# Two casts moved in the start-up of an attention and swish kernel: one v cast ahead of two evacuations on ScalarE, one weight cast from GpSimd to VectorE

## Chip, cores, metric

The kernel runs on one core of one Trainium2 chip. The metric is the device time of one execution in microseconds (us). Before the change it is 283.29 us, the median of 3 runs (283.11 to 283.29). The execution that the profiler took was a slower one, 283.81 us.

## The reference, cut to what matters

```python
# attention, 8 batches x 8 heads, 576 rows, head_dim 64
q_s = exp(q - max(q)) ; q_s = q_s / (sum(q_s, -1) + 1e-9)
k_s = exp(k - max(k, 2)) ; k_s = k_s / (sum(k_s, 2) + 1e-9)
kv  = einsum('bhsd,bhse->bhde', k_s, v)
x   = einsum('bhsd,bhde->bhse', q_s, kv)       # then (4608, 512)
# swish layer, d_model 512, d_ff 2048
h = x @ w_in
g = h * (1 / (1 + exp(-beta * h)))
out = g @ w_out                                # float32
```

## The kernel before: the parts concerned

TensorE computes, batch by batch, `h = x @ w_in` (line 457) and `acc = g @ w_out` (line 509). While the weights are still arriving, batch 0 is worked; then the attention of batch 1 is prepared. All weights and inputs arrive as fp32 and are cast to bf16, in the order in which SyncE issues their transfers:

```python
    for k0 in range(4):
        load_w_in(0, k0, k0 + 1)
    for blk in range(1, 4):
        load_w_in(blk, 0, 2)           # 512 KB: k-slices 0 and 1
        load_w_in(blk, 2, 4)           # 512 KB: k-slices 2 and 3
    for j0 in range(0, NJ, 2):
        load_w_out(j0)
    # ... cut
    for blk in range(1, 4):
        for k0 in (0, 2):
            cast_w_in(blk, k0, nc.gpsimd)      # two casts of 128x512
    for j0 in range(0, NJ, 2):
        cast_w_out(j0, nc.gpsimd)
        if j0 == 6:
            # loads of batch 1: q (2), then k, v, v for each half (g)
```

The preparation of batch 1. `b_mm(m)` puts m matmuls of `g @ w_out` between the steps:

```python
    def batch_1():
        b_mm(32)
        eq_exp(1, 0)                     # ScalarE: exp of q, first half
        eq_exp(1, 1)
        eq_sum(1, 0)                     # VectorE: reduce, reciprocal
        eq_div(1, 0, nc.vector)          # VectorE: divide
        for c in range(2):
            ek_exp(1, 0, c)              # ScalarE: exp of k
        b_mm(20)
        eq_sum(1, 1)
        eq_t(1, 0, "X0", None)           # TensorE: "first transposes"
        ev_cast(1, 0, 0, nc.gpsimd)
        ev_cast(1, 0, 1, nc.scalar, 0, 4)
        ev_cast(1, 0, 1, nc.gpsimd, 4, KT9)
        eq_div(1, 1, nc.vector)
        for c in range(2):
            ek_exp(1, 1, c)
        b_mm(3)
        ekv_mm(1, 0, ("H0", "H1"))       # TensorE: first kv group
        b_mm(1)
        eq_t(1, 1, "H2", None)           # TensorE: "second transposes"
        ekv_rk(1, 0)                     # VectorE
        ekv_norm(1, 0, (nc.vector, nc.scalar))
        eq_out(1, 0, nc.vector)          # VectorE: copy of qT
        # ... v casts of the second half, eq_out(1, 1)
        b_mm(4)
        x_group(1, (0,), ["X0", "H0"])   # TensorE
        ekv_mm(1, 1, ("X1", "K"))        # second kv group
        # ... cut; after it the h matmuls of batch 1 begin
```

Finishing a stripe inside `b_mm` also puts its evacuation (line 538, `o<-acc`) into ScalarE's program. The order in which these calls stand is the order in which each engine works.

The softmax here doesn't subtract the row's maximum and nothing guards it: scores larger than these inputs give would overflow.

Of the kernel before, what the change touches and what calls it, by code (L numbers as in the profile page):

```python
# [16 lines left out]
def kernel(  # L17
# [10 lines left out]
    nc = tc.nc  # L28
# [7 lines left out]
    CH = 512  # L36
# [24 lines left out]
    def bank(n, shape, dtype, name):  # L61
        return banks[n].tile(shape, dtype, tag=n, name=name)
# [13 lines left out]
    w_in_b = const.tile([P, KT, FF], BF16, name="w_in_b")  # L76
# [73 lines left out]
    def cast(eng, dst, src):  # L150
        if eng is nc.scalar:
            nc.scalar.copy(dst, src)  # L152
        elif eng is nc.gpsimd:
            if len(src.shape) > 3:
                for i in range(src.shape[1]):
                    cast(eng, dst[:, i], src[:, i])
                return
            n = 1
            for d in src.shape[1:]:
                n *= d  # L160
            nc.gpsimd.affine_select(  # L161
                out=dst, in_=src, pattern=[[0, n]], base=0, channel_multiplier=0,
                compare_op=ALU.is_equal, fill=fill0,
            )
        else:
            eng.tensor_copy(dst, src)  # L166

    def cast_w_in(blk, k0, eng, m0=0, m1=CH):
        t, k1 = ld["wi", blk, k0]
        for k_ in range(k0, k1):  # L170
            cast(eng, w_in_b[:, k_, blk * CH + m0 : blk * CH + m1], t[:, k_ - k0, m0:m1])
# [18 lines left out]
    def eq_exp(b, g):  # L190
        if b not in Eq:
            Eq[b] = atn.tile([P, 2, 2 * NT, 2, D], BF16, tag="Eq", name=f"Eq{b}")
            qz[b] = atn.tile([P, 2, 2 * NT, 2], F32, tag="qz", name=f"qz{b}")
        nc.scalar.activation(  # L194
            Eq[b][:, g].rearrange("p m c d -> p c m d"),
            ld["q", b, g].rearrange("p (c a) (t d) -> p c (a t) d", c=2, t=NT),
            ACTF.Exp,
        )

    def eq_sum(b, g):  # L200
        nc.vector.tensor_reduce(qz[b][:, g], Eq[b][:, g], axis=AX.X, op=ALU.add)  # L201
        nc.vector.reciprocal(qz[b][:, g], qz[b][:, g])

    def eq_div(b, g, eng):
        eng.tensor_tensor(
            Eq[b][:, g],
            Eq[b][:, g],
            qz[b][:, g].unsqueeze(3).to_broadcast((P, 2 * NT, 2, D)),
            ALU.mult,
        )  # L210

    def eq_t(b, g, n, eng):
        if b not in qT:
            qT[b] = atn.tile([P, 2, 2, NT, P], BF16, tag="qT", name=f"qT{b}")
        ps = bank(n, [P, 2 * NT, P], BF16, f"tp{b}_{g}")
        for m in range(2 * NT):
            nc.tensor.transpose(  # L217
                ps[:, m, :], Eq[b][:, g, m].rearrange("p c d -> p (c d)"), ident[:]
            )
        tps[b, g] = ps  # L220
        if eng is not None:
            eq_out(b, g, eng)
# [4 lines left out]
    def ek_exp(b, g, c):  # L227
        if b not in Ek:
            Ek[b] = atn.tile([P, KT9, 2, 2, D], BF16, tag="Ek", name=f"Ek{b}")
        nc.scalar.activation(  # L230
            Ek[b][:, :, g, c],
            ld["k", b, g][:, c].rearrange("p (t d) -> p t d", d=D),
            ACTF.Exp,
        )

    def ve(b):
        return va[b][:, 0 : 2 * KT9].rearrange("p (t g) n -> p t g n", g=2)

    def ev_cast(b, g, c, eng, t0=0, t1=KT9):
        cast(  # L240
            eng,
            ve(b)[:, t0:t1, g, c * VH : c * VH + D],
            ld["v", b, g][:, c, t0 * D : t1 * D].rearrange("p (t d) -> p t d", d=D),
        )
# [21 lines left out]
    def ekv_rk(b, g):  # L266
        for a in range(2):
            j = 2 * g + a
            rks[b, j] = atn.tile([P, 1], F32, tag=f"rk{j}", name=f"rks{b}_{j}")
            nc.vector.reciprocal(rks[b, j][:], ekv[b, j, 0][:, D : D + 1])  # L270
# [12 lines left out]
    def x_out(b, kt, eng):  # L283
        cast(eng, xT[b][:, kt], xps[b, kt][:])
# [207 lines left out]
    def cols(n, st):  # L492

        if n == NCH - 1 and st > 2:
            return ((0, DM // 2), (DM // 2, 3 * DM // 4), (3 * DM // 4, DM))[st - 3]
        return 0, DM

    def b_mm(m):
        while m and pos[0] < len(bq):
            n, st, j = bq[pos[0]]  # L500
            if n * NJ + j + LAG + (n == 1 and j < 4) > done_a[0] and done_a[0] < NCH * NJ - 1 and n:
                break
            if j == 0:
                name = ("X1", "K", "A0", "A1")[st] if n == 0 else f"A{st % 2}"
                if st == 5:
                    name = "X0"
                acc[n, st] = bank(name, [P, DM], F32, f"acc{n}_{st}")
            c0, c1 = cols(n, st)
            nc.tensor.matmul(  # L509
                acc[n, st][:, c0:c1],  # L510
                gs[n, j][:, min(st, 3) * P : (min(st, 3) + 1) * P],
                w_out_b[:, j, c0:c1],
                start=(j == 0),
                stop=(j == NJ - 1),
            )
            if j == NJ - 1 and (n, st) != (0, 3):
                store(n, st)
            pos[0] += 1
            m -= 1

    def store(n, st):
        o = osp.tile([P, DM], F32, tag="o", name=f"o{n}_{st}")
        if n == NCH - 1 and st > 2:
            rows = out[(B - 1) * S : (B - 1) * S + CH, :].rearrange("(p t) e -> p t e", t=NT)
            c0, c1 = cols(n, st)
            if st < 5:
                nc.vector.tensor_scalar(
                    o[:, c0:c1], acc[n, st][:, c0:c1], 0.5, None, op0=ALU.mult
                )
                nc.sync.dma_start(rows[:, 3, c0:c1], o[:, c0:c1])  # L530
            else:
                nc.scalar.activation(o[:, c0:c1], acc[n, st][:, c0:c1], ACTF.Copy, scale=0.5)
                nc.scalar.dma_start(rows[:, 3, c0:c1], o[:, c0:c1])
            return
        if n == 0 and st == 3:
            nc.vector.tensor_scalar(o[:], acc[n, st][:], 0.5, None, op0=ALU.mult)
        else:
            nc.scalar.activation(o[:], acc[n, st][:], ACTF.Copy, scale=0.5)  # L538
        if n == TC:
            for m in range(2):  # L540
                b = 2 * st + m
                nc.sync.dma_start(out[b * S + CH : (b + 1) * S, :], o[m * R : (m + 1) * R])
        else:
            b = n if n < TC else B - 1
            rows = out[b * S : b * S + CH, :].rearrange("(p t) e -> p t e", t=NT)
            nc.sync.dma_start(rows[:, st, :], o[:])
# [87 lines left out]
        unit_mm(0, i, 2, 3)  # L634
    for blk in range(1, 4):
        for k0 in (0, 2):
            cast_w_in(blk, k0, nc.gpsimd)
    for j0 in range(0, NJ, 2):
        cast_w_out(j0, nc.gpsimd)
        if j0 == 6:  # L640
# [13 lines left out]
    def batch_1():  # L654
        b_mm(32)
        eq_exp(1, 0)
        eq_exp(1, 1)
        eq_sum(1, 0)
        eq_div(1, 0, nc.vector)
        for c in range(2):  # L660
            ek_exp(1, 0, c)
        b_mm(20)
        eq_sum(1, 1)
        eq_t(1, 0, "X0", None)
        ev_cast(1, 0, 0, nc.gpsimd)
        ev_cast(1, 0, 1, nc.scalar, 0, 4)
        ev_cast(1, 0, 1, nc.gpsimd, 4, KT9)
        eq_div(1, 1, nc.vector)
        for c in range(2):
            ek_exp(1, 1, c)  # L670
        b_mm(3)
        ekv_mm(1, 0, ("H0", "H1"))
        b_mm(1)
        eq_t(1, 1, "H2", None)
        ekv_rk(1, 0)
        ekv_norm(1, 0, (nc.vector, nc.scalar))
        eq_out(1, 0, nc.vector)
        ev_cast(1, 1, 0, nc.gpsimd)
        ev_cast(1, 1, 1, nc.vector, 0, 3)
        ev_cast(1, 1, 1, nc.scalar, 3, 6)  # L680
        ev_cast(1, 1, 1, nc.gpsimd, 6, KT9)
        eq_out(1, 1, nc.vector)
        b_mm(4)
        x_group(1, (0,), ["X0", "H0"])
        ekv_mm(1, 1, ("X1", "K"))
        x_out(1, 0, nc.scalar)
        ekv_rk(1, 1)
        ekv_norm(1, 1, (nc.vector, nc.scalar))
        x_out(1, 1, nc.vector)
        b_mm(4)  # L690
        store(0, 3)
        x_group(1, (1,), ["H1", "H2"])
        for i in range(4):
            unit_mm(1, i, 0, 1)
        x_out(1, 2, nc.scalar)
        x_out(1, 3, nc.vector)
        for i in range(4):
            unit_mm(1, i, 1, 2)
        for m in range(4):
            q_exp(2, m)  # L700
        unit_mm(1, 4, 0, 2)
        for i in range(5):
            unit_mm(1, i, 2, 3)
        for m in range(3):
            q_norm(2, m)
# [94 lines left out]
```

## Time and profile before

| | before |
|---|---|
| median, range | 283.29 us, 283.11 to 283.29 |
| span of the profiled execution (283.81 us on the clock of the runs) | 282.1 us |
| TensorE | 97% busy, granted clock 1.000 |
| transfers moved from 0 to 42 us | 242 to 406 GB/s, close to saturated |
| two gaps of TensorE that the change aims at | 20.2 to 20.95 us, 42.0 to 42.49 us |

A timeline line gives start, length, engine, source line, operation, output and input tiles, shapes, count and, in brackets, the idle time ahead of it with what ended it. The lines themselves stand in the prediction.

### The profile page before, as it was taken

What the parts mean: (1) busy time and instruction counts of PE and PEld (TensorE: products, weight loads), DVE (VectorE), ACT (ScalarE), POOL (GpSimd) and SP (SyncE); (2) the same over time, 40 slices, a digit from 0 to 9 for tenths busy, and PEclk for the clock granted to TensorE, in tenths of its full rate; (3) what the DMA queues carried; (4) which work ended last, traced back from release to release, by engine and by line L of the source; (5) the groups of instructions that cost most, each with busy time, mean ns of one, the idle gap of its engine ahead of it and who ended that gap; (6) DMA issues with size and microseconds to landing.
All of it is one profiled execution on the core that took longest, in us unless ns stands there. A gap on an engine that the chain in (4) does not pass through costs nothing.

```text
span 282.1 us, 4611 instructions
## 1 busy us (share of the span) xinstructions
PE 273.7 (97%) x1664; PEld 136.2 (48%) x1692; DVE 155.5 (55%) x282; ACT 168.1 (60%) x280; POOL 70.5 (25%) x120
## 2 busy tenths in 40 slices
PE   7989999999999999999999999999999999999995
PEld 3545445545444445444444444444444444444444
DVE  2947359976865485638564766466453333444401
ACT  4856367867965587457854785478454544444411
POOL 3368831450631054104510361027000000000000
PEclk9999999999999999999999999999999999999999
DMA  7999999889799908991699069904200200031112
GB/s 242 371 392 406 388 385 359 291 141 359 176 202 354 209 37 183 326 230 64 141 315 285 34 143 305 279 32 110 79 37 2 76 37 37 2 76 37 40 74 74
DMA packets 51559, 51.69 MB, mean 183 GB/s; under 512 B 21068, under 2 KB 41932, under 8 KB 51536
## 3 DMA queue, kind: packets, MB, share of 16 engines
q1 hardware_dynamic: 51360, 51.33, 60.9%
q8 instruction: 13, 0.21, 0.3%
q14 instruction: 10, 0.08, 0.1%
q10 hardware_dynamic: 144, 0.07, 0.1%
q0 software_dynamic: 32, 0.01, 0.0%
HBM read 38.28 MB, written 9.44 MB: 169 GB/s over the span
## 4 chain that ended last, share of the span: by engine, by line
PE 83%; DMA 13%; ACT 1%; issue 1%; SPq 1%; ACTq 0%
PE acc L509 40%; PE h L457 39%; DMA k<-in_k_dram 7%; DMA wo<-in_moe_w_out_dram 3%; DMA wi<-in_moe_w_in_dram 3%; PE kv L384 2%; PE x L408 2%; PE kv L259 0%; ACT Ek L230 0%; SPq L105 0%; ACT o L538 0%; SPq L117 0%; PE xt L422 0%; PE tp L217 0%; ACT va L152 0%
## 5 line engine op out<-in xcount | busy, mean ns | idle before, releaser
L471 DVE SCALAR_TENSOR_TENSOR g<-th,h 128x512 bf16<-128x512 bf16 x144 | 97.3, 685 | 98.5 <-ACT th L469 98.2
L469 ACT ACTIVATE th<-h,beta_h 128x512 bf16<-128x512 f32 x144 | 97.1, 689 | 85.7 <-PE h L457 82.7
L509 PE MATMUL acc<-w_out_b,g 128*128 128x512 bf16 (+2 forms) x590 | 142.8, 368 | 1.7 <-issue 1.1
L457 PE MATMUL h<-xT,w_in_b 128*128 128x512 bf16 x503 | 127.6, 379 | 1.0 <-POOL w_in_b L161 0.4
L457 PEld LDWEIGHTS <-w_in_b 128*128 128x128 bf16 x576 | 64.8, 113 | 61.9 <-POOL w_in_b L161 1.4
L509 PEld LDWEIGHTS <-g 128*128 128x128 bf16 x608 | 56.9, 98 | 63.9 <-issue 2.5
L315 POOL TENSOR_TENSOR Eq<-Eq,qz 128x512 bf16<-128x512 bf16 x24 | 25.1, 1049 | 84.3 <-issue 41.0
L538 ACT ACTIVATE o<-acc 128x512 f32<-128x512 f32 x34 | 20.0, 591 | 8.9 <-PE acc L509 7.4
L161 POOL TENSOR_SCALAR_AFFINE_SELECT va<-v 128x256 bf16<-128x256 f32 (+3 forms) x55 | 21.6, 427 | 13.8 <-DMA v<-in_v_dram 13.5
L355 ACT ACTIVATE Ek<-k 128x640 bf16<-128x640 f32 x24 | 17.7, 737 | 0.0
L457 PE MATMUL h<-xTt,w_in_b 128*128 128x512 bf16 x63 | 16.4, 379 | 0.1
L313 DVE TENSOR_REDUCE qz<-Eq 128x8 f32<-128x512 bf16 x24 | 16.2, 675 | 0.0
L305 ACT ACTIVATE Eq<-q 128x512 bf16<-128x512 f32 x24 | 14.7, 623 | 0.0
L201 DVE TENSOR_REDUCE qz<-Eq 128x16 f32<-128x1024 bf16 x4 | 4.9, 1216 | 10.8 <-ACT Eq L194 10.8
L166 DVE CAST xT<-x 128x512 bf16<-128x512 f32 x15 | 10.3, 685 | 0.6 <-PE x L408 0.5
L582 PE MATMUL warm<-zf 128*128 128x512 f32 (+1 forms) x14 | 9.0, 778 | 1.5 <-DVE zf L549 1.5
L161 POOL TENSOR_SCALAR_AFFINE_SELECT w_in_b<-wi 128x512 bf16<-128x512 f32 x16 | 9.5, 612 | 3.9 <-DMA wi<-in_moe_w_in_dram 3.8
L152 ACT CAST xT<-x 128x512 bf16<-128x512 f32 x17 | 9.7, 578 | 0.8 <-PE x L408 0.7
L194 ACT ACTIVATE Eq<-q 128x1024 bf16<-128x1024 f32 x4 | 4.2, 1056 | 9.5 <-DMA q<-in_q_dram 9.5
L341 POOL TENSOR_TENSOR Et<-Et,zt 128x512 bf16<-128x512 bf16 x4 | 4.2, 1042 | 21.0 <-DVE zt L340 21.0
L161 POOL TENSOR_SCALAR_AFFINE_SELECT w_out_b<-wo 128x1024 bf16<-128x1024 f32 x8 | 8.3, 1039 | 1.9 <-DMA wo<-in_moe_w_out_dram 1.8
L408 PE MATMUL x<-qT,kvn 64*64 64x512 bf16 x64 | 6.0, 391 | 0.4 <-ACT xT L152 0.4
(52 smaller groups left out, 78.3 us busy)
## 6 DMA issues: line engine op xcount, KB each, us to landing
q<-in_q_dram SPq DMA_DIRECT2D x16, 512.0 KB, 6.2
out_dram<-o SPq DMA_DIRECT2D x31, 256.0 KB, 3.1
k<-in_k_dram SPq DMA_DIRECT2D x24, 320.0 KB, 7.5
v<-in_v_dram SPq DMA_DIRECT2D x24, 320.0 KB, 7.5
wo<-in_moe_w_out_dram SPq DMA_DIRECT2D x8, 512.0 KB, 10.4
wi<-in_moe_w_in_dram SPq DMA_DIRECT2D x6, 512.0 KB, 9.7
k<-in_k_dram SPq DMA_DIRECT2D x4, 576.0 KB, 8.8
v<-in_v_dram SPq DMA_DIRECT2D x6, 288.0 KB, 8.6
```

Source lines behind the costliest of these rows:

```text
L161: nc.gpsimd.affine_select(out=dst, in_=src, pattern=[[0, n]], base=0, channel_multiplier=0, compare_op=ALU.is_equal, fill=fill0,)
L166: eng.tensor_copy(dst, src)
L305: nc.scalar.activation(by_pair(Eq[b], m).rearrange("p t h d -> p h t d"), ld["q", b, hf][:, a : a + 2, :].rearrange("p h (t d) -> p h t d" ...
L313: nc.vector.tensor_reduce(z, e, axis=AX.X, op=ALU.add)
L315: nc.gpsimd.tensor_tensor(e, e, z.unsqueeze(3).to_broadcast((P, NT, 2, D)), ALU.mult)
L355: nc.scalar.activation(Ek[b][:, :, h0:h1, :].rearrange("p t h d -> p h t d"), ld["k", b, hf][:, a : a + h1 - h0, :].rearrange("p h (t d) - ...
L408: nc.tensor.matmul(xps[b, 2 * g + c][o, :], kvn[b][r, j, :], qT[b][r, g, a] if b < EARLY else qT[b][r, :, j, :], start=True, stop=True,)
L457: nc.tensor.matmul(hs[n, i][:], w_in_b[:, kt, blk * CH + r : (blk + 1) * CH : 4], rhs_a(n, kt), start=(kt == 0), stop=(kt == KT - 1),)
L469: nc.scalar.activation(th[:], h[:], ACTF.Tanh, scale=beta_h[:, i // 4, i % 4 : i % 4 + 1])
L471: nc.vector.scalar_tensor_tensor(out=g[:], in0=th[:], scalar=1.0, in1=h[:], op0=ALU.add, op1=ALU.mult)
L509: nc.tensor.matmul(acc[n, st][:, c0:c1], gs[n, j][:, min(st, 3) * P : (min(st, 3) + 1) * P], w_out_b[:, j, c0:c1], start=(j == 0), stop=(j ...
L538: nc.scalar.activation(o[:], acc[n, st][:], ACTF.Copy, scale=0.5)
```

## The change

The intent is to take two short waits off TensorE. Part A: of the second piece of w_in's block 1, VectorE casts k-slice 3 while GpSimd casts slice 2. Part B: ScalarE casts the last piece of v ahead of two evacuations of `acc`, not behind them.

```diff
         for k0 in (0, 2):
-            cast_w_in(blk, k0, nc.gpsimd)
+            if (blk, k0) == (1, 2):
+                t, _ = ld["wi", 1, 2]
+                cast(nc.gpsimd, w_in_b[:, 2, CH : 2 * CH], t[:, 0])
+                cast(nc.vector, w_in_b[:, 3, CH : 2 * CH], t[:, 1])
+            else:
+                cast_w_in(blk, k0, nc.gpsimd)
@@ batch_1 @@
-        b_mm(20)
+        b_mm(6)
+        ev_cast(1, 0, 1, nc.scalar, 0, 4)
+        b_mm(14)
         eq_sum(1, 1)
         eq_t(1, 0, "X0", None)
         ev_cast(1, 0, 0, nc.gpsimd)
-        ev_cast(1, 0, 1, nc.scalar, 0, 4)
         ev_cast(1, 0, 1, nc.gpsimd, 4, KT9)
```

## The prediction

> **What bounds the kernel now.** I read the head of the page first, to see which engine sets the time.
>
> ```profile
> span 282.1 us, 4611 instructions
> PE 273.7 (97%) x1664; PEld 136.2 (48%) x1692; DVE 155.5 (55%) x282; ACT 168.1 (60%) x280; POOL 70.5 (25%) x120
> DMA  7999999889799908991699069904200200031112
> ```
>
> TensorE is busy for 273.7 of 282.1 us, at a granted clock of 1.000, so both parts of the change can only win TensorE's idle time: 8.4 us in the whole run. The DMA digits of 9 in the first six slices (7.05 us each) are the second limit: while the weights and batch 1 arrive, the transfers are saturated. The list of all waits names the two gaps at which the change aims:
>
> ```profile
> PE h L457 <- POOL w_in_b L161: 0.4, 2, 0.2
> PE kv L259 <- ACT va L152: 0.3, 1, 0.3
> ```
>
> The timeline of TensorE from 12.5 us shows where the first lies, and that of GpSimd shows why:
>
> ```profile
> 15.03 5.13 PE L457 MATMUL h<-xT,w_in_b 128*128 128x512 bf16 x23 [0.17 <-issue]
> 20.39 0.41 PE L457 MATMUL h<-xT,w_in_b 128*128 128x512 bf16 x1 [0.23 <-POOL w_in_b L161]
> ...
> 19.72 1.18 POOL L161 TENSOR_SCALAR_AFFINE_SELECT w_in_b<-wi 128x512 bf16<-128x512 f32 x2 [1.72 <-DMA wi<-in_moe_w_in_dram]
> 21.06 1.18 POOL L161 TENSOR_SCALAR_AFFINE_SELECT w_in_b<-wi 128x512 bf16<-128x512 f32 x2 [0.17 <-DMA wi<-in_moe_w_in_dram]
> ```
>
> GpSimd stood idle for 1.72 us until the piece landed at about 19.7, then cast its two k-slices one after the other (612 ns each): slice 2 ready at 20.33, slice 3 at 20.90. TensorE waits for each: one matmul at 20.39, the next at 20.95. Its displayed ends are modelled; from starts, 24 matmuls at 0.216 us from 15.03 give 20.21 as the next free slot, so 0.18 us is lost before slice 2 and 0.56 - 0.216 = 0.34 before slice 3.
>
> The second gap is in the preparation of batch 1. All engines, 36.8 to 45.6 us:
>
> ```profile
> 36.90 1.06 ACT L194 ACTIVATE Eq<-q 128x1024 bf16<-128x1024 f32 x1 [6.18 <-DMA q<-in_q_dram]
> 37.99 1.22 DVE L201 TENSOR_REDUCE qz<-Eq 128x16 f32<-128x1024 bf16 x1 [6.49 <-ACT Eq L194]
> 39.53 1.23 DVE L205 TENSOR_TENSOR Eq<-Eq,qz 128x1024 bf16<-128x1024 bf16 x1
> 40.70 1.21 POOL L161 TENSOR_SCALAR_AFFINE_SELECT va<-v 128x576 bf16<-128x576 f32 x2 [4.21 <-DMA v<-in_v_dram]
> 40.91 0.61 PE L217 MATMUL tp<-ident,Eq 128*128 128x128 bf16 x8
> 41.07 1.06 ACT L538 ACTIVATE o<-acc 128x512 f32<-128x512 f32 x2
> 42.02 0.41 ACT L152 CAST va<-v 128x256 bf16<-128x256 f32 x1
> 42.21 1.22 DVE L205 TENSOR_TENSOR Eq<-Eq,qz 128x1024 bf16<-128x1024 bf16 x1
> 42.49 0.69 PE L259 MATMUL kv<-va,Ek 64*128 64x131 bf16 x18 [0.33 <-ACT va L152]
> 43.11 0.39 PE L509 MATMUL acc<-w_out_b,g 128*128 128x512 bf16 x1
> 43.49 0.62 PE L217 MATMUL tp<-ident,Eq 128*128 128x128 bf16 x8
> 44.16 0.69 DVE L166 COPY qT<-tp 128x1024 bf16<-128x1024 bf16 x1
> 44.91 0.73 PE L408 MATMUL x<-qT,kvn 64*64 64x512 bf16 x4
> ```
>
> The reader is to see two things. ScalarE's cast (42.02 to 42.43) sits behind two evacuations (1.06 us), and TensorE's kv group starts at 42.49, right after it. But VectorE, woken at 37.99 by a q transfer that landed at 36.9, works without a gap until 45.83, and TensorE's transposes start just after its two divisions end (40.76 gives 40.91; 43.43 gives 43.49), as the x group starts just after the copy of qT ends (44.85 gives 44.91). **VectorE's stream, started by the DMA, is the clock of this stage.** The cast is only the last wait in front of one group that lies between two of its ticks.
>
> **What the Trainium skill says.** "TensorE: Matmul & The Clock Gate", the specification table at its head, gives the three other compute engines strict first-in-first-out queues of 8. So the new VectorE cast, which comes before the first multiply (g of unit 0) in that engine's program, will hold that multiply until its transfer has landed. The trace before agrees with in-order engines (the ScalarE cast did wait behind the evacuations). "SBUF — State Buffer", section "Who interferes with whom", says a VectorE copy or cast in a two-port mode takes a port pair that GpSimd also needs, for the whole instruction, and the other engine blocks. "VectorE: DVE Perf Modes", section "The perf-mode tier table", gives 1227 ns for 2048 fp32 elements in SBUF at two per cycle of 0.96 GHz; taking off 1536 elements at 0.52 ns, my estimate for 512 is 0.43 us. No large SBUF cast on VectorE is in this trace (one of 192 elements took 353 ns; 512 from PSUM 685 ns), so mode and lock remain open until the run.
>
> **Part A, the w_in cast.** One 612 ns cast leaves GpSimd; one of about 0.43 us (0.69 at worst) is added to VectorE, beside it. Three cases for the piece that lands at 19.7:
> - No blocking: slice 2 is ready at 20.33 and slice 3 at 20.15. TensorE runs both back to back, 0.34 us earlier.
> - GpSimd first: slice 3 is ready at 20.33 + 0.43 = 20.76 in place of 20.90: 0.14 us.
> - VectorE first: slice 3 at 20.15, slice 2 only at 20.15 + 0.61 = 20.76. The first matmul starts at about 20.82, the second at 21.03, 0.08 us later than now.
>
> The other side of A is the multiplies. In the trace they start at 18.54; the blocked queue lets the first start only at 20.2 (or 20.8). They run at 0.62 us a unit, so g of unit 7, behind seven others and one small operation of 0.5 us, ends about 5.5 us later: 25.7 (or 26.3). It frees the bank into which unit 12 goes. TensorE reaches unit 12 at 20.95 + 23 x 0.216 = 25.92 now, 25.58 in the first case. So there A gives back about 0.15 us, and in the second case 0.5. At 29.4 I expect TensorE between 0.4 us later and 0.3 earlier, most likely 0.1 to 0.2 earlier. GpSimd itself gains nothing: it waits about 0.2 us for each following piece.
>
> And then this is lost: 52 matmuls later TensorE stands before the transposes of Eq, which start at 40.91 because the division ends at 40.76. Now it is free at 29.39 + 52 x 0.216 = 40.62, already 0.29 us early. Being earlier lengthens that wait; being up to 0.29 later only shortens it. **A is worth 0.00 at 40.91.**
>
> **Part B, the v cast.** Nothing is added: the order on ScalarE becomes exp, exp, cast, evacuation, evacuation. The cast runs from about 41.07 to 41.48 instead of 42.02 to 42.43. GpSimd's two v casts end at 41.91, the three matmuls before the kv group leave TensorE free at 41.35 + 3 x 0.216 = 42.00. So kv starts at about 42.0 in place of 42.49: 0.49 us won locally. It takes 0.62 us, one matmul follows (0.22), and at 42.84 TensorE meets the second transposes, whose division still ends at 43.43: it waits 0.65 us there, and starts at 43.49 as before. The two evacuations end at 42.5 as before, in front of an exp that waits for its k transfer until 42.92. **B is worth 0.00 at 43.49.** The sum is 0.0; small shifts downstream (the kv reciprocals are behind the second division in VectorE's queue, so they don't move) I put at 0.1 us.
>
> **Rivals.** First, both gains arrive: 0.34 + 0.49 = 0.8 us, 282.5. The wait list speaks for it, as it blames ScalarE and GpSimd; the ends on VectorE just before 43.49 and 44.91 speak against it. Only a quicker q transfer could move those, and the transfers run at 385 to 406 GB/s whatever the casts do: neither part issues one earlier. Second, the late multiplies become the bound: banks come free 0.5 us or more too late, TensorE passes 40.91 late by more than B's new slack of 0.65 us. That needs almost a microsecond of delay, three times my worst case; it would give 283.5 to 284. Third, the port lock keeps slice 2 back (the third case of A): locally a loss of 0.08, at the end nothing, 283.2.
>
> **Range and chances.** Mechanism says 283.29 less 0 to 0.2; runs before spread over 0.18 us. I say 283.15, with 282.75 below (half of the local gains arrive) and 283.45 above (a bank wait leaks through). A 2% change would be 5.7 us, more than half of all TensorE idle time: 0.5% on each side.
>
> **What would show it.** Right: kv near 42.0 and no wait for the ScalarE cast before it; TensorE idle 0.5 to 0.65 us before the second transposes, which start within 0.1 us of 43.49; x at 44.9; the first multiply at 20.2 to 20.8 behind the VectorE cast. The cast's own length and the start of GpSimd's tell whether they block each other. Wrong: second transposes or x group 0.3 us earlier than now, or a TensorE wait for a multiply near 25.9 that is still there at 43.5.

## The result, and the profile after

The changed kernel takes 283.38 us (median of 4 runs, 283.2 to 283.72) beside 283.29 us before (4 runs by now, 283.11 to 283.45). The ratio is 1.0005 with a 95% interval of 0.9988 to 1.0022. Ratios here and below are the mean time of one kernel's runs over that of the other's of the same rounds, so not quite the ratio of the medians quoted. Executions over 1.5% slower than the fastest of the same kernel are left out of the means.

The head of the page after, and the two lines of its list of waits that answer to the two gaps (engine, line, releaser, us in total, times, longest):

```profile
span 282.0 us, 4639 instructions
PE 276.2 (98%) x1692; PEld 136.3 (48%) x1692; DVE 155.7 (55%) x283; ACT 168.3 (60%) x280; POOL 70.1 (25%) x119
```

```profile
PE tp L217 <- DVE Eq L205: 0.7, 2, 0.4
...
PEld L457 <- POOL w_in_b L161: 0.5, 1, 0.5
```

The rise of TensorE's busy time is not more work: the trace before lacks some matmul records (1664 against 1692). The two waits of before (on POOL and on ACT's `va`) are gone from the list of TensorE's matmuls, and a new one stands there: transposes that wait for VectorE's division of Eq. The wait for the cast of w_in is not gone altogether: one is left in the list of weight loads (PEld).

The timelines of the stage of part A, after (TensorE's matmuls and weight loads, VectorE, GpSimd):

```profile
15.16 11.60 PE L457 MATMUL h<-xT,w_in_b 128*128 128x512 bf16 x52
...
20.52 5.97 PEld L457 LDWEIGHTS <-w_in_b 128*128 128x128 bf16 x29 [0.47 <-POOL w_in_b L161]
...
19.57 0.43 DVE L166 CAST w_in_b<-wi 128x512 bf16<-128x512 f32 x1 [3.58 <-DMA wi<-in_moe_w_in_dram]
19.92 4.26 DVE L471 SCALAR_TENSOR_TENSOR g<-th,h 128x512 bf16<-128x512 bf16 x7
...
19.61 0.86 POOL L161 TENSOR_SCALAR_AFFINE_SELECT w_in_b<-wi 128x512 bf16<-128x512 f32 x1 [1.69 <-DMA wi<-in_moe_w_in_dram]
```

TensorE's matmuls are drawn as one row, but a wait is left in it: 24 of them at 0.216 us from 15.16 end at 20.34, and the weights of slice 2 are loaded only at 20.52, so 0.18 us is lost there; slice 3 follows one matmul later. VectorE's cast takes the 0.43 us of my estimate. GpSimd's cast beside it takes 0.86 us in place of 0.612. The multiplies start at 19.92, behind the cast, in place of 18.54.

The stage of part B, after, all engines:

```profile
36.84 1.06 ACT L194 ACTIVATE Eq<-q 128x1024 bf16<-128x1024 f32 x1 [6.33 <-DMA q<-in_q_dram]
...
40.85 0.61 PE L217 MATMUL tp<-ident,Eq 128*128 128x128 bf16 x8 [0.27 <-DVE Eq L205]
...
41.35 0.41 ACT L152 CAST va<-v 128x256 bf16<-128x256 f32 x1 [0.25 <-DMA v<-in_v_dram]
...
41.66 1.08 ACT L538 ACTIVATE o<-acc 128x512 f32<-128x512 f32 x2
...
42.03 0.69 PE L259 MATMUL kv<-va,Ek 64*128 64x131 bf16 x18
42.15 1.22 DVE L205 TENSOR_TENSOR Eq<-Eq,qz 128x1024 bf16<-128x1024 bf16 x1
...
43.43 0.62 PE L217 MATMUL tp<-ident,Eq 128*128 128x128 bf16 x8 [0.39 <-DVE Eq L205]
...
44.85 0.73 PE L408 MATMUL x<-qT,kvn 64*64 64x512 bf16 x4
```

The cast is ahead of the evacuations and the kv group starts at 42.03 in place of 42.49. The second transposes start at 43.43 in place of 43.49, and that 0.06 is exactly what the q transfer was earlier in this execution (36.84 for 36.90). The won 0.46 us now stands as idle time ahead of the transposes. The chain of waits after (start, us, what) shows the same from behind; before, its piece at this place ran over k's transfer, the evacuations and the v cast:

```profile
26.33 10.49 DMA q<-in_q_dram
...
36.84 1.07 ACT Eq L194
...
42.15 1.24 DVE Eq L205
...
43.43 0.62 PE tp L217 x8
```

### The profile page after: what moved, and what is told of

Its sections match the earlier page's. It is cut to its first block, busy times and chain, and to the rows that moved or that the text cites. A ratio compares the mean times of both kernels' runs of the same rounds, so it can differ in the third digit from the quotient of the medians.

```text
span 282.0 us, 4639 instructions
## 1 busy us (share of the span) xinstructions
PE 276.2 (98%) x1692; PEld 136.3 (48%) x1692; DVE 155.7 (55%) x283; ACT 168.3 (60%) x280; POOL 70.1 (25%) x119
## 4 chain that ended last, share of the span: by engine, by line
PE 84%; DMA 11%; DVE 2%; SPq 1%; ACT 0%; issue 0%; POOL 0%; ACTq 0%
PE acc L509 40%; PE h L457 39%; DMA wo<-in_moe_w_out_dram 4%; DMA q<-in_q_dram 4%; DMA wi<-in_moe_w_in_dram 3%; PE kv L384 2%; PE x L408 2%; DVE Eq L205 1%; DVE qz L201 1%; SPq L105 1%; ACT Eq L194 0%; SPq L117 0%; PE xt L422 0%; POOL w_in_b L161 0%; PE kv L259 0%
## 5 line engine op out<-in xcount | busy, mean ns | idle before, releaser
L509 PE MATMUL acc<-w_out_b,g 128*128 128x512 bf16 (+2 forms) x608 | 145.5, 368 | 0.0
L582 PE MATMUL warm<-zf 128*128 128x512 f32 (+1 forms) x14 | 9.6, 824 | 1.5 <-DVE zf L549 1.5
```

What stands on the lines that cost most here:

```text
L509: nc.tensor.matmul(acc[n, st][:, c0:c1], gs[n, j][:, min(st, 3) * P : (min(st, 3) + 1) * P], w_out_b[:, j, c0:c1], start=(j == 0), stop=(j ...
```

## The experiments

My theory: VectorE's stream in batch 1, started by the q transfer, is the clock of that stage, so local gains of TensorE ahead of its ticks become idle time. Rivals: each part gains and the other part spoils it; or no time was freed at all. Unless told otherwise a run has 5 timed rounds. "Before" in the same rounds was 283.27 us for the first four, 283.35 us for the next four, 283.48 us for the last.

### Each part alone

`a_only` has only the first hunk of the diff, `b_only` only the second.

> Part A alone (one w_in cast on VectorE). Theory (VectorE's stream, started by the q transfer, is the clock of batch 1's preparation): TensorE comes to its first w_out matmul 0.2 to 0.3 us earlier than in the kernel before, then waits longer in front of the transposes of Eq; these start at 40.9 within 0.1 us, the second ones at 43.5, and the time is that of before within 0.1 us. Rival 1 (the gain of 0.3 us arrives): 283.0. Rival 2 (A's later multiplies cost what part B wins, which is why the sum is nothing): 283.6 or more, and a TensorE wait for a multiply near 25.5.

> Part B alone (the v cast ahead of two evacuations). Theory: the kv group starts near 42.0 in place of 42.49, the second transposes at 43.5 as before, with 0.4 to 0.6 us of TensorE idle ahead of them; time as before within 0.1 us. Rival 1 (the gain arrives): 282.8. Rival 2 (A spoils B): faster than before by 0.3 us or more, and faster than A alone.

Measured: 283.36 us (ratio 1.0001, 0.9988 to 1.0013) and 283.30 us (1.0001, 0.9987 to 1.0015). Neither gains, neither costs, so it isn't that one spoils the other. The profiled executions seem to contradict: the span of `b_only` is 281.4 us, 0.7 under before. Its timeline tells why (ScalarE's first exp of q, then TensorE's second transposes):

```profile
36.25 1.06 ACT L194 ACTIVATE Eq<-q 128x1024 bf16<-128x1024 f32 x1 [5.41 <-DMA q<-in_q_dram]
...
42.84 0.62 PE L217 MATMUL tp<-ident,Eq 128*128 128x128 bf16 x8
```

The q transfer came 0.65 us earlier in that execution. Set beside each other, the four traces are one and the same from q on:

| start, us | before | after | a_only | b_only |
|---|---|---|---|---|
| exp of q (transfer landed) | 36.90 | 36.84 | 36.54 | 36.25 |
| second transposes, after q | 6.59 | 6.59 | 6.59 | 6.59 |
| h matmuls of batch 1, after q | 10.68 | 10.68 | 10.63 | 10.67 |
| span, less the start of q's exp | 245.2 | 245.2 | 245.2 | 245.2 |

With or without A or B, the time of these four executions is the landing of q plus a constant, to 0.05 us, and the landing moves by some tenths between executions by itself. (k and v come in the same stream of transfers, so the table alone does not tell which of them holds the stage; the next experiment does.) A comparison of spans would have "shown" a gain of 0.7 us for part B. One expectation missed: in `b_only` TensorE waits not 0.4 to 0.6 but only 0.08 us ahead of the second transposes (42.54 + 0.216 = 42.76, start 42.84), because q was early and TensorE itself late: its first transposes started only when its own 52 matmuls were over, at 29.51 + 52 x 0.216 = 40.74. TensorE's slack in this stage is thus between 0.1 and 0.55 us from one execution to the next.

### VectorE's stream made longer

`sum_twice_after`, the changed kernel:

```diff
+        nc.vector.tensor_reduce(qz[1][:, 1], Eq[1][:, 1], axis=AX.X, op=ALU.add)
         eq_sum(1, 1)
```

> The changed kernel with VectorE's second reduction of Eq (1.21 us) done twice; the result is the same. Theory: VectorE's stream is the clock, so the second transposes move from 43.43 to 44.65, the x group from 44.85 to 46.05, and the time rises by all of 1.2 us, to 284.5. Rival (TensorE, ScalarE or the k transfer is the clock and VectorE has slack like TensorE's 0.6 us): a rise of 0.6 us or less.

Measured: 284.25 us against 283.35 (1.0034, 1.0021 to 1.0046), so +0.9 where the theory said 1.2 and the rival at most 0.6. The trace gives the missing piece. From the landing of q (36.40) the second transposes stand at 7.83 (+1.24, all of it), the x group at 45.65 - 36.40 = 9.25 (+1.24), but the second kv group at 9.64 in place of 8.67 (+0.97). In the kernel before, the x group is halted halfway for ScalarE's normalisation, whose place in ScalarE's stream hangs on k's transfer (weight loads in the trace of before):

```profile
45.23 0.11 PEld L408 LDWEIGHTS <-kvn 64*64 64x64 bf16 x3 [0.22 <-ACT kvn L279]
```

With everything later that halt is gone (the x group takes 0.41 for 0.73 us). So VectorE's stream sets the second transposes and the start of the x group, but not the end of the stage: there ScalarE's stream, held by k's transfer, was the later one, and VectorE had 0.27 us of slack (1.24 less 0.97). The table above agrees: `a_only`'s h matmuls come 0.05 us sooner after q, but counted from the exp of k's second half (42.92, 42.86, 42.51 and 42.25) they start 4.66 or 4.67 us later in all four.

### TensorE made the later one

`pad6_*` puts six needless matmuls ahead of the second transposes, `pad10_*` ten ahead of the first, in both kernels:

```diff
+    def pad(n, m):
+        ps = bank(n, [P, CH], F32, f"pad{m}")
+        for _ in range(m):
+            nc.tensor.matmul(ps[:], ident[:], w_out_b[:, 0, :], start=True, stop=True)
 ...
+        pad("X0", 10)                      # pad10
         eq_t(1, 0, "X0", None)
 ...
         b_mm(1)
+        pad("H2", 6)                       # pad6
         eq_t(1, 1, "H2", None)
```

> The kernel before, with six needless matmuls (1.30 us of TensorE) ahead of the second transposes, so that TensorE and not VectorE is the later one there. Theory: TensorE is free at 43.33, so the transposes move from 43.5 to 44.6, the x group from 44.9 to 45.9, the second kv group from 45.57 to 46.4; the time is 0.8 us above before, 284.1.

> The changed kernel with the same six matmuls. Theory: TensorE was free at 42.87 there, so the transposes go to 44.2, the x group to 45.5, the second kv group to 46.0; the time is 0.4 us above before, 283.7, so 0.45 us faster than the padded kernel before: part B's gain was there as slack and shows as soon as TensorE is the later one. Rival (part B frees no time on TensorE, or gives it back elsewhere): the two padded kernels take the same time.

Measured: 284.32 (1.0036, 1.0024 to 1.0049) and 284.22 us (1.0034, 1.0021 to 1.0046). Their means differ by 0.07 us; the spread of the ten runs makes that -0.1 to 0.25 by my estimate (95%), so the expected 0.45 is a miss. In the traces, TensorE in `pad6_before`, then in `pad6_after`:

```profile
42.08 0.69 PE L259 MATMUL kv<-va,Ek 64*128 64x131 bf16 x18 [0.16 <-ACT va L152]
...
44.44 0.61 PE L217 MATMUL tp<-ident,Eq 128*128 128x128 bf16 x8 [0.27 <-DVE qT L166]
```

```profile
41.83 0.69 PE L259 MATMUL kv<-va,Ek 64*128 64x131 bf16 x18
...
44.19 0.61 PE L217 MATMUL tp<-ident,Eq 128*128 128x128 bf16 x8 [0.27 <-PE acc L509]
```

The h matmuls follow at 48.20 and 47.95. All of the 0.25 us between them stands in front of the kv group already. In `pad6_before` that group still waits for ScalarE's v cast, whose stream follows k's transfer; in `pad6_after` it waits for nothing but TensorE's own matmuls. So part B's gain in this pair is 0.25 us. (The two executions had q at 36.49 and 36.64, so counted from q the h matmuls start at 11.71 and 11.31; but that 0.40 is no fair count, as TensorE in `pad6_after` does not hang on q: its first transposes start at 40.64, right after its own 52 matmuls from 29.40.) This is seen in one pair of traces and not proved by the times. (The padding itself cost about 0.2 us more than its matmuls, in both: the transposes into the same bank start 1.51 us after it, not 1.30.)

> The kernel before with ten needless matmuls (2.16 us) ahead of the first transposes. Theory: TensorE was free at 40.62, so these go from 40.91 to 42.8, the kv group to 43.9, the second transposes to 44.7, the second kv group to 46.45; 0.9 us above before, 284.2.

> The changed kernel with the same ten matmuls. TensorE is later than every other engine up to the x group in both, so only part A's gain can show, and part B's can't. Theory: everything 0.2 to 0.34 us earlier than in the padded kernel before: first transposes 42.5, time 283.9 to 284.0. Rival (A gains nothing on TensorE): the same time.

Measured: 285.12 (284.52 to 285.42; 1.0058) and 285.21 us (285.1 to 285.27; 1.0063). Two misses. The cost is 1.8 us and not 0.6 to 0.9, because I had left out that once TensorE leads, VectorE's reciprocals, normalisation and copy of qT must follow the kv group (they end at 46.73 in `pad10_before`, and the x group starts at 46.78). And part A gains nothing that the times show (the means differ by 0.13 us the wrong way, within the spread). The traces say why: the piece of w_in was cast from 18.92 and 18.60, long before TensorE wanted it, so there was no wait to remove (h matmuls from 16.11 and 15.86 without a gap). I looked at the ten traces taken so far. The cast of this piece begins at 19.5 to 19.7 in before, after and `a_only`, and at 18.4 to 18.9 in the seven others, where TensorE, which then starts its h matmuls up to a microsecond later, has no wait for slices 2 and 3. **The wait that part A attacks is that of some executions**; of the four traces without part A, only that of before has it. The 0.2 us by which after's first w_out matmul was earlier than before's (29.19 for 29.39) was luck to the larger part: part A's share is the 0.07 us found next.

### Part A where its wait always exists

The piece is loaded two transfers later (order 1/0, 2/0, 2/2, 1/2, 3/0, 3/2), in the kernel before, in the changed one, and in one in which VectorE takes slice 2 and GpSimd slice 3. One look each, so state unknown; only the traces are read.

```diff
-    for blk in range(1, 4):
-        load_w_in(blk, 0, 2)
-        load_w_in(blk, 2, 4)
+    for blk, k0 in ((1, 0), (2, 0), (2, 2), (1, 2), (3, 0), (3, 2)):
+        load_w_in(blk, k0, k0 + 2)
 ...                                        # late_swap only:
-                cast(nc.gpsimd, w_in_b[:, 2, CH : 2 * CH], t[:, 0])
-                cast(nc.vector, w_in_b[:, 3, CH : 2 * CH], t[:, 1])
+                cast(nc.vector, w_in_b[:, 2, CH : 2 * CH], t[:, 0])
+                cast(nc.gpsimd, w_in_b[:, 3, CH : 2 * CH], t[:, 1])
```

> The traces so far show that the wait which part A attacks is there in some executions only: the piece landed at 19.7 in the profile of before, but at 18.9 in that of the padded kernels before, where TensorE had no wait. Here the piece is loaded two transfers later (about 22.2), so TensorE always waits for it. The kernel before in this form, counted from the start of GpSimd's first cast of the piece (S): slice 2 is used at S + 0.67, slice 3 at S + 1.23, as in the profile of before.

> The changed kernel with the late piece. Theory (the two engines block each other: VectorE's cast takes 0.43 us, GpSimd's is stretched from 0.61 to 0.86): slice 2 used at S + 0.91, slice 3 right after it at S + 1.13: part A gains 0.1 us where its wait exists, not the 0.34 that I predicted for the case without blocking. Rival (no blocking, the 0.86 had another cause): S + 0.67 and S + 0.88.

> As the one before, but VectorE casts slice 2, which is used first, and GpSimd slice 3. With blocking as told: slice 2 used at S + 0.45, slice 3 when GpSimd's stretched cast is over, S + 0.91: 0.3 us gained against the kernel before. Without blocking: slice 3 at S + 0.67.

TensorE at the first use of slice 2, in `late_before`, `late_after` and `late_swap`:

```profile
22.50 0.41 PE L457 MATMUL h<-xT,w_in_b 128*128 128x512 bf16 x1 [1.99 <-POOL w_in_b L161]
23.07 1.25 PE L457 MATMUL h<-xT,w_in_b 128*128 128x512 bf16 x3 [0.16 <-POOL w_in_b L161]
```

```profile
23.35 0.97 PE L457 MATMUL h<-xT,w_in_b 128*128 128x512 bf16 x2 [2.35 <-POOL w_in_b L161]
```

```profile
22.15 1.09 PE L457 MATMUL h<-xT,w_in_b 128*128 128x512 bf16 x3 [1.14 <-DVE w_in_b L166]
```

GpSimd's first cast began (S) at 21.84, 22.43 and 21.70. So slice 2 is used at S + 0.66, S + 0.92 and S + 0.45. Slice 3 is used at S + 1.23 in the first. In the second its weights are loaded together with those of slice 2 (two loads from 23.34), but its matmul starts only at 23.68, S + 1.25, as TensorE's clock is already falling there (0.75 from 23 to 24 us). At the full clock, in the traces of after and `a_only`, it starts one matmul after slice 2, at S + 1.16. In the third the weights are loaded at 22.61, S + 0.91. So the casts are as expected: GpSimd's beside VectorE's took 0.86 us again, part A gains 0.07 us where its wait exists, and giving VectorE the slice that is needed first gains 0.3. The times (286.50, 287.01, 284.37 us, one run each) must not be compared for this: the long waits of the first two were followed by half of TensorE's clock (last section), that of the third was not.

### Moving the clock itself

If VectorE's stream is what counts, shorten it. (The diffs of this part are against the changed kernel, and cut.) `q_ahead` issues the first q transfer two w_out pieces earlier, shares the last w_out cast between GpSimd and ScalarE, brings the first transposes and the qT copy forward, and gives VectorE ScalarE's share of one normalisation:

```diff
         load_w_out(j0)
+        if j0 == 10:
+            load_q(1, 0)
 ...
-        cast_w_out(j0, nc.gpsimd)
+        if j0 < 14:
+            cast_w_out(j0, nc.gpsimd)
+        else:
+            cast(nc.gpsimd, w_out_b[:, 14], ld["wo", 14][:, 0])
 ...
         eq_exp(1, 0)
+        cast(nc.scalar, w_out_b[:, 15], ld["wo", 14][:, 1])
 ...
-        b_mm(14)
+        b_mm(6)
+        eq_t(1, 0, "X0", nc.vector)
+        b_mm(8)
 ...
-        ekv_norm(1, 0, (nc.vector, nc.scalar))
-        eq_out(1, 0, nc.vector)
+        ekv_norm(1, 0, (nc.vector, nc.vector))
```

> The changed kernel with VectorE's stream in batch 1 relieved: the first q transfer is issued two w_out pieces earlier (those land 1.3 us later, the last one's cast is shared by GpSimd and ScalarE), the first transposes and the copy of qT come earlier, and VectorE does ScalarE's share of one normalisation. Theory: the second division ends at about 42.6 in place of 43.43, the x group starts at 44.1 in place of 44.85, the second kv group at about 44.9 in place of 45.51, held by the last v transfer; time 0.6 us below before, 282.7. If the stage is held elsewhere: no gain, or a loss of up to 0.5 us where the late w_out pieces stop TensorE at 37.4.

Measured: 283.35 us (0.9994, 0.998 to 1.0008): no gain. VectorE, GpSimd and TensorE in its timeline:

```profile
36.74 1.22 DVE L205 TENSOR_TENSOR Eq<-Eq,qz 128x1024 bf16<-128x1024 bf16 x1
...
36.77 1.67 POOL L161 TENSOR_SCALAR_AFFINE_SELECT w_out_b<-wo 128x512 bf16<-128x512 f32 x1 [0.28 <-DMA wo<-in_moe_w_out_dram]
...
38.49 1.45 PE L509 MATMUL acc<-w_out_b,g 128*128 128x512 bf16 x6 [0.85 <-POOL w_out_b L161]
```

GpSimd's cast began 0.03 us after VectorE's division, which reads two tensors from SBUF, and took 1.67 us in place of 0.61; TensorE stood for 0.85 us. The second attempt, `q_ahead2`, keeps GpSimd away from that piece and lets the qT copy follow the second division (what it shares with `q_ahead` is left out):

```diff
         eq_exp(1, 0)
+        cast(nc.scalar, w_out_b[:, 15], ld["wo", 14][:, 1])
         eq_exp(1, 1)
         eq_sum(1, 0)
+        cast(nc.vector, w_out_b[:, 14], ld["wo", 14][:, 0])
         eq_div(1, 0, nc.vector)
 ...
+        eq_out(1, 0, nc.vector)
         ekv_rk(1, 0)
-        ekv_norm(1, 0, (nc.vector, nc.scalar))
-        eq_out(1, 0, nc.vector)
+        ekv_norm(1, 0, (nc.vector, nc.vector))
```

> The first attempt to relieve VectorE (q_ahead) lost its gain to a blocked cast: GpSimd's 512 elements of w_out took 1.67 us beside VectorE's division, and TensorE stood for 0.85 us. Here GpSimd has no part of that piece: VectorE casts one half ahead of its division, ScalarE the other, and the copy of qT follows the second division. Theory: no TensorE wait for w_out, second transposes at 42.7, x group at 44.0, second kv group at about 45.1 in place of 45.57, now held by the casts of the last v transfer (lands near 44.6); h of the next part starts 0.4 us earlier against the q transfers' own time; time 0.4 us below before. If the last v transfer or TensorE holds it more than I think: 0 to 0.2 us.

Measured: 283.12 us (283.03 to 283.26) against 283.48: ratio 0.9988, 0.9974 to 1.0002, so perhaps a gain of 0.3 us, not sure by the interval. In the trace there is no wait for w_out and the second transposes start right behind TensorE's own matmul. The stage's end is now tied to something else (VectorE and TensorE):

```profile
44.19 0.35 DVE L166 CAST va<-v 128x192 bf16<-128x192 f32 x1 [0.46 <-DMA v<-in_v_dram]
...
44.69 0.69 PE L259 MATMUL kv<-va,Ek 64*128 64x131 bf16 x18 [0.18 <-POOL va L161]
```

The h matmuls start 7.52 us after the first exp of k (46.69 less 39.17), in place of 7.67 before and after: 0.15 us won. Three engines wait here for the last v transfer, which lands 5.02 us after k's exp began; in the trace of before GpSimd was working on that same piece 4.5 us after it. Why it lands later against k in this order I can't say; no run settles it.

## Why the prediction was right

Step by step, as it was put:

- **The time**: 283.38 us lies inside 282.75 to 283.45, and there was no 2% change. I had put 0.1 to 0.2 us of small gains into the number; nothing of that is seen. The range ends 0.07 us above the median, and single runs of the changed kernel spread over 0.5 us (283.2 to 283.72), so that the median fell inside is in part luck; that nothing was gained is not.
- **VectorE's stream is the clock**: right for the second transposes and the start of the x group, which is where part B's gain was lost. They kept their distance from q to 0.01 us in four traces with and without the parts, and lengthening VectorE's stream by 1.2 us lengthened the time by 0.9. The missing 0.3 shows that the end of the stage had another clock, which the sum left out: ScalarE's share of the normalisation, behind k's transfer, came 0.27 us later than VectorE's stream. Neither part moved that either, so the result is the same.
- **Part B worth 0.49 locally and 0.00 at the end**: right. It measured 0.46 in front of the kv group. The cast ran from 41.35 to 41.76 and not from 41.07, as its v piece had only just landed, but TensorE's own matmuls (41.29 + 3 x 0.216 = 41.94) were the later ones, as predicted. TensorE then waited 0.55 us by starts (42.66 + 0.216 to 43.43) where I had said 0.65.
- **Part A, the three cases**: none of them occurred as written. I had the two engines either side by side or strictly one after the other. In fact GpSimd's cast starts and is stretched by 0.25 us, so slice 2 comes 0.25 late and slice 3 is there already: 0.07 us gained, against my 0.34, 0.14 and -0.08. And in most executions the wait isn't there at all, which one trace of the kernel before, of an execution 0.5 us above the median, could not tell me. The 0.29 us of slack at the first transposes, on which I put the loss of A's gain, is of that execution too: in `b_only` and `pad6_before` TensorE comes to them from its own matmuls without a wait. The 0.00 for A is right, but in those executions for another reason: there is no wait to remove.
- **The late multiplies**: they started at 19.92 (I said 20.2 to 20.8), and the one that frees unit 12's bank ended at 24.92 in place of my 25.7. The cast was over 0.28 us sooner than I said, and I had carried over the 0.50 us of the small operation in front of it from before; it took 0.23 this time, and it has between 0.23 and 0.68 in the traces. TensorE's bank wait did not come.
- **The rivals**: none came. No local gain arrived in the time, and no bank wait leaked through.
- **Slips in the working, without effect**: the 8.4 us of TensorE's idle time are too many, as the trace before lacks matmul records; the trace after, with as many matmuls as weight loads (1692), leaves 5.8 (282.0 less 276.2). The first of the six DMA digits is a 7. And a delay of almost a microsecond (0.94) is 2.4 times the worst case of 0.4, not three times.

## What to carry to other kernels

Before removing a wait, find the next thing that its waiter will meet, and what that hangs on: here the 0.46 us saved in front of one group was waited off in front of the next, less than a microsecond later, as that one's input was fixed by a transfer. When executions differ by a few tenths, count times from the event that starts the stage, once you have seen that the stage does hang on it; the distance is then steady to hundredths where the span moves by 0.7 us. And look at several executions before attacking a wait: the late landing behind one of the two here is in three traces out of ten.

## What the Trainium skill lacked or had wrong

- "SBUF — State Buffer", section "Who interferes with whom", says that a VectorE operation in a two-port mode, and one with two inputs in SBUF, contends with a GpSimd one that reads SBUF, and of the first kind that whichever issues first holds the ports for the whole instruction and the other fully blocks. The direction agrees. Beside a two-input VectorE multiply of 1.22 us, GpSimd's cast took 1.67 us in place of 0.61; beside a 0.43 us VectorE cast that began 0.03 to 0.04 us earlier it took 0.86, nine times alike. VectorE's cast took 0.43 with and without company (`q_ahead2`'s w_out cast, GpSimd idle). A block to the end of VectorE's instruction would have added 1.19 and about 0.4 us; measured are 1.06 and 0.25, both 0.13 to 0.15 us less. So the page's block fits here but for that last part of VectorE's instruction. Nor does the page say where a profile shows the blocked time: here as a longer GpSimd instruction, and not as idle time in front of it.
- "TensorE: Matmul & The Clock Gate", section "Why this matters for your kernels", asks for no TensorE gap above about 3 us. Here a wait of 1.99 us was followed by half the clock. Windows of `late_before` (us, then busy time and count of PE, PEld, DVE, ACT and POOL, granted clock, DMA share, GB/s):

```profile
24.00:26.00 2.00, 2.00 (x6) 0.73 (x5) 1.45 (x3) 1.57 (x3) 2.00 (x5) 0.50 1.01 406
```

  A wait of 2.35 us in `late_after` was followed by the same (0.50 from 24 to 26 us); one of 1.14 us in `late_swap` left it at 1.00. Where between the limit lies, these runs don't show.
- No page has it that the landing of one and the same transfer moves by up to 0.65 us between executions of kernels that are alike ahead of it (36.25 to 36.90 for q), which is more than the whole change was worth.
